# The planner's clocks, the zero products' limit and the per-stretch settings of a two-layer attention and MLP kernel

## The chip, the cores and the metric

The kernel runs on one core of one Trainium2 chip. The metric is the device time of one execution in microseconds. Four engines share the work: TensorE (PE in the profile) for matrix products, ScalarE (ACT) for exponentials and tanh, VectorE (DVE) for elementwise work, GpSimd (POOL) for integer additions. SyncE (SP) issues the DMAs.

## The reference

The input x has 2048 rows of 512 bfloat16 values. Two layers are run with the same weights. Each layer is an attention block and an MLP block, both with a residual:

```python
x = x + _A_ref(_layernorm(x, axis=-1), A_wqkv, A_wo)   # 32 heads of 16, softmax over 2048 keys
x = x + _B_ref(_layernorm(x, axis=-1), B_w1, B_w2)     # 512 -> 1792, silu, -> 512
x = x + _A_ref(_layernorm(x, axis=-1), A_wqkv, A_wo)
x = x + _B_ref(_layernorm(x, axis=-1), B_w1, B_w2)
```

Inside `_A_ref` the scores are `q k / 4`, softmax is taken over all keys, and the heads' outputs are joined and multiplied by `wo`. The heads are so narrow (16 columns) that the exponentials, 2 x 32 x 2048 x 2048 of them, are the bulk of the work.

## The kernel before, in words

**Tiles and segments.** The queries are cut into 4 chunks of 512 and the heads into 8 groups of 4 (`hb`). A segment (`Seg`) is one layer, one chunk and one group of heads. It walks over 16 blocks of 128 keys, and each block gives two tiles (`pr` 0 and 1, two heads each), so a full segment has 32 tiles. In the second layer some segments are split: an "old" part over 12 key blocks (24 tiles), which can begin before the last chunk of the first layer is finished, and a "new" part over the last 4 (8 tiles). There are 74 segments and 2048 tiles: 1024 in layer 0 (chunks 0 to 3 one after another), then 240 in "old" parts, 272 in the rest of chunks 0 and 1 of layer 1, and 512 in chunks 2 and 3 of layer 1.

**One tile.** TensorE writes the scores of a tile into one of three PSUM slots (L1282). Then one of two ways makes the exponentials. Either ScalarE does it in one activation (L1497). Or VectorE does it: one multiply-add that makes the bit pattern of a rough power of two (L1531), and three shifted copies of that pattern, whose sum smooths it. Each copy is an integer addition, done on GpSimd (L1592) or on VectorE (L1565). A ScalarE tile needs one pair of value products on TensorE (L1358), a VectorE tile four such pairs, one for each copy. The value products of a segment add up in a single PSUM bank, `o_ps`. When all are done the bank is copied out (`close`, L1176 to L1184), and only then may the next segment's value products begin. Until then its exponentials wait in SBUF buffers, of which there are 14 and some lent ones.

**Background work.** Everything else (keys, queries, values, layer norm, output projection, MLP) is cut into `Piece`s: lists of steps, each with an engine, a planned duration in ns and a function. Two pieces matter here. `k_piece` ends with `k_out`, a VectorE step that writes keys into `KT` (planned at 302 ns, L321). `heads_piece` divides the heads' outputs by their sums: after a DMA transpose of `oT` into the single buffer `at`, one VectorE step `heads_norm` issues a reciprocal of the sums (L513) and a product over all values (L514). It is planned as one step of 640 ns (one group of heads) or 920 ns (two groups). There are 42 such pieces. The kernel's `ending` calls `heads_norm` once more.

**The order.** The order of instructions on TensorE, ScalarE, VectorE and GpSimd is fixed when the program is built. Class `Flow` plays the kernel on a model: each engine has a clock (`self.pe`, `self.act`, `self.dve`, `self.pool`), the engine with the earliest clock takes a turn, and instructions are written in the order in which the model issues them. A planned duration is therefore not a time on the chip; it only changes the order. Two clocks model the waiting of VectorE and GpSimd for one another: `self.lock` is the end of GpSimd's last planned addition, `self.held_port` the end of the last VectorE step marked "l". A VectorE step marked "l" is planned not before `self.lock`, and GpSimd's next addition not before `self.held_port`.

**Which tile goes to VectorE.** `want_dve` (L1248) says so for each tile as its scores are issued. Before, only tiles issued as a pair (two free slots at once) could go; not those of the last four positions of a segment (`left < LAST`, 5); not with more than `behind` additions pending; not with fewer than `spare` free buffers; not two tiles in direct succession. Those two numbers, and others, come from a letter: `RULES` has 128 letters, one for each 16 tiles, and `KINDS` gives each letter's numbers as (spare, many, few, behind, hurry, help, wait). `help` and `wait` say when VectorE makes shifted copies itself, `hurry` scales how fast background work is fed in.

**Zero products.** Where TensorE would be idle in the plan, `warm` (L1379) inserts a product with a matrix of zeros (L1393), if the planned busy share of the last 3300 ns is at most `WARM`, 0.65. They add nothing to a result.

Of the kernel before, what the change touches and what calls it, by code (L numbers as in the profile page):

```python
# [12 lines left out]
FP32 = mybir.dt.float32  # L13
# [7 lines left out]
def kernel(  # L21
# [14 lines left out]
    S, D = xf.shape  # L36
    F = B_w1.shape[-1]
    P = 128
    H = 32
    DH = D // H  # L40
# [224 lines left out]
    def dve(ns, fn, g=""):  # L265
        return ("dve", ns, fn, g)
# [62 lines left out]
    def k_piece(L, c, hb):  # L329
        cell = {}  # L330

        def out():
            st = cell["st"] = stpool.tile([P, 512], BF16, name="kq", tag="kq")
            nc.vector.tensor_copy(out=st[:], in_=cell["ps"][:, :])  # L334
            move(kept_q[L, hb, c, :, :], st[:])

        p = Piece(four(
            lambda cts: k_mm(c, hb, cell["ps"][:, :], cts),
            lambda: bank(cell, "k_ps"),
        ) + [dve(700, out, "c"), dve(302, lambda: k_out(c, hb, cell["st"][:]), "l")])  # L340
        p.key = (L, c, hb)
        p.store = Piece([])
        return p
# [163 lines left out]
        return fetch, f  # L507


    def heads_norm(at_ps, hb, attn):  # L510
        n = at_ps.shape[2]
        rec = bmpool.tile([P, 4, 8, 1], FP32, name="rec", tag="rec")[:, :, 0:n, :]
        nc.vector.reciprocal(rec, at_ps[:, :, :, DH : DH + 1])  # L513
        nc.vector.tensor_tensor(  # L514
            out=attn[:, :, 64 * hb : 64 * hb + DH * n].rearrange("p t (j d) -> p t j d", j=n),
            in0=at_ps[:, :, :, 0:DH],
            in1=rec.to_broadcast([P, 4, n, DH]),
            op=ALU.mult,
        )

# [2 lines left out]
    def heads_piece(oT, seg, attn):  # L523
        alone = seg.c < 2 and (seg.L == 1 or seg.hb < 2)
        alone = alone or (seg.L, seg.c, seg.hb) == (1, NQC - 1, HB - 2)
        k = 0 if alone else seg.hb % 2
        if k == 0:
            at_cell["at"] = opool.tile([P, 4, 2, P], BF16, name="at", tag="at")
        at = at_cell["at"]
        turn(at[:, :, k, :], oT[:])  # L530
        if not alone and k == 0:
            return None
        n = 4 * (k + 1)
        heads = at[:].rearrange("p t s (j w) -> p t (s j) w", j=4)[:, :, 0:n, :]
        return Piece([dve(640 if k == 0 else 920, lambda: heads_norm(heads, seg.hb - k, attn))])

    def o_transpose(a_ps, attn, tq):
        for ct in range(CT):
# [115 lines left out]
    def ending(oT, attn, slots, units):  # L654
# [24 lines left out]
        for tq, k in units[4:10]:  # L679
            tail_mm(slots, tq, k)  # L680
        warm(max(0, 5 - len(units[4:])))
        heads_norm(at_ps, hb, attn)
        a_ps = gpool.tile([P, 4, P], BF16, name="a4_ps", tag="g")
        for tq in range(4):
            nc.tensor.transpose(a_ps[:, tq, :], attn[:, tq, (CT - 1) * P : D], ident[:, :])
# [117 lines left out]
    first = [0]  # L803
# [136 lines left out]
    class Flow:  # L940
# [36 lines left out]
        def rule(self, n):  # L977
            letter = RULES[n // STRETCH]
            (
                self.spare, self.many, self.few, self.behind, self.hurry, self.help, self.wait,  # L980
            ) = KINDS[letter]

        def landed(self, at):
# [262 lines left out]
            return max(self.end + 916 * (j + 1), t.at + 490 + 1017) + 50  # L1246

        def want_dve(self, t, at, two):  # L1248
            if not two or t.n < 4 or t.n - self.last_dve < 2:
                return False  # L1250
            left = 2 * len(t.seg.kts) - 2 * (t.kt - t.seg.kts[0]) - t.pr
            if left < LAST or len(self.zs) > 0 or len(self.passes) > self.behind:
                return False
            if sum(b[0] <= at + 600 for b in self.bufs) - self.owed() < self.spare:
                return False
            if sum(len(l) for l in self.lanes) > ROWS:
                return False
            return self.dve < at + 475 + LATE
# [356 lines left out]

    SWITCH, T_PASS, T_BITS, T_SHIFT = 100, 1225, 430, 1000

    LAST, ROWS, LATE, EVEN = 5, 20, 900, 0
    SPAN, WARM = 3300, 0.65
    STRETCH = 16  # L1620
    KINDS = {
        "a": (5, 6, 2, 3, 1.0, 2, 100), "b": (3, 6, 2, 3, 1.0, 2, 100), "c": (4, 6, 2, 3, 1.0, 2, 100),
        "d": (6, 6, 2, 3, 1.0, 2, 100), "e": (8, 6, 2, 3, 1.0, 2, 100), "f": (99, 6, 2, 3, 1.0, 2, 100),
        "g": (5, 4, 2, 3, 1.0, 2, 100), "h": (5, 9, 2, 3, 1.0, 2, 100), "i": (5, 6, 1, 3, 1.0, 2, 100),
        "j": (5, 6, 3, 3, 1.0, 2, 100), "k": (5, 6, 2, 2, 1.0, 2, 100), "l": (5, 6, 2, 5, 1.0, 2, 100),
        "m": (5, 6, 2, 6, 1.0, 3, 100), "n": (5, 6, 2, 6, 1.0, 3, 400), "o": (5, 6, 2, 4, 1.0, 3, 300),
        "p": (5, 6, 2, 3, 1.4, 2, 100), "q": (5, 6, 2, 3, 0.7, 2, 100), "r": (99, 6, 2, 3, 1.5, 2, 100),
        "s": (5, 6, 2, 3, 1.4, 3, 100), "t": (5, 6, 2, 3, 1.0, 3, 100), "u": (5, 6, 2, 3, 1.0, 1, 100),
        "v": (5, 6, 2, 3, 1.0, 2, 300), "w": (4, 6, 2, 6, 1.0, 3, 400), "x": (7, 6, 2, 6, 1.0, 3, 400),
        "y": (5, 4, 2, 6, 1.0, 3, 400), "z": (5, 6, 2, 6, 1.4, 3, 400), "A": (5, 9, 2, 6, 1.0, 3, 400),  # L1630
        "B": (5, 6, 2, 6, 0.7, 3, 400), "C": (5, 6, 3, 6, 1.0, 3, 400),
    }
    RULES = (
        "bbbbbbbbmmmmmmmmwwwwwwwwwwwwwwwwppppppppbbbbbbbbddddddddcccccccc"
        "aaaaaaaakkkkkkkknnnnnnnnvvvvvvvvwwwwwwwwwwwwwwwweeeeeeeellllllll"
    )
    TAU, NEAR, URGENT, HARD = 700, 300, 4000, 6000
    FROM, TO, EARLY = 0, 99, 300
# [155 lines left out]
```

## Time and profile before

| what | value |
|---|---|
| median of 3 runs | 1624.14 us (1622.63 to 1628.64) |
| time of the profiled execution | 1620.71 us |
| its span, first to last instruction | 1618.9 us |
| ACT busy, PE busy | 1557.0 us and 1546.3 us (96% each) |
| POOL busy, DVE busy | 1293.6 us (80%) and 1239.8 us (77%) |
| mean granted clock of TensorE | 0.991 |
| tiles on ScalarE (L1497) and on VectorE (L1531) | 1596 and 452 |
| shifted copies on GpSimd (L1592) and VectorE (L1565) | 1203 and 153 |
| zero products of the plan (L1393) | 211 |

Busy times are shares of the span of one execution. TensorE's matmuls overlap and their ends are modelled, so its 96% is not a measure of how full it is. An instruction's duration includes the time that it waits for a shared port, which matters for VectorE and GpSimd here. A wait is put down to the engine that released it.

### The profile page before, as it was taken

The page shows a single profiled execution, that of the slowest core. Times are in us where ns is not written, and L with a number is a line of the kernel's source. Part 1 is how long each engine was busy: PE and PEld are TensorE (multiplying, and loading weights), DVE is VectorE, ACT ScalarE, POOL GpSimd, SP SyncE. Part 2 cuts the span into 40 slices and gives each one's busy share as a digit, 9 for nine tenths or more (in the row PEclk, how much of TensorE's full clock was granted, in tenths as well). Part 3 has the DMA queues.
Part 4 walks back from the last instruction along what each step waited for, and adds up shares of the span by engine and source line. Part 5 has one row for each costly group of instructions (what it writes and reads, how often), then busy time and mean ns, then how long its engine had stood idle before and what let it go on. Part 6 is the DMA issues. An engine that isn't in the chain of part 4 may idle for free.

```text
span 1618.9 us, 41459 instructions
## 1 busy us (share of the span) xinstructions
PE 1546.3 (96%) x16750; PEld 477.4 (29%) x16756; DVE 1239.8 (77%) x1550; ACT 1557.0 (96%) x1767; POOL 1293.6 (80%) x1349
## 2 busy tenths in 40 slices
PE   8999999999999999999999999998999999999998
PEld 3322222233322323233222232222223222222333
DVE  7898888876777678658987668886878887777764
ACT  6999999999999999999999998998999999999993
POOL 3899998987898778868777866876879998889880
PEclk9999999999999999999999999998999999999999
DMA  5011101100210011001120011112100110010000
GB/s 195 21 40 37 30 23 27 27 11 11 37 23 11 11 27 41 11 14 33 57 59 23 14 27 35 37 35 45 30 11 17 33 27 14 18 33 18 17 24 14
DMA packets 105744, 49.24 MB, mean 30 GB/s; under 512 B 79024, under 2 KB 105040, under 8 KB 105552
## 3 DMA queue, kind: packets, MB, share of 16 engines
q1 hardware_dynamic: 103536, 45.51, 11.0%
q8 instruction: 131, 2.15, 0.6%
q10 hardware_dynamic: 2016, 1.08, 0.2%
q14 instruction: 61, 0.50, 0.1%
HBM read 17.20 MB, written 11.27 MB: 18 GB/s over the span
## 4 chain that ended last, share of the span: by engine, by line
PE 59%; ACT 22%; DVE 11%; issue 6%; POOL 2%; DMA 1%; ACTq 0%; DVEq 0%; POOLq 0%
PE slot L1282 21%; PE q_ps L1358 19%; ACT p L1497 15%; PE y_ps L312 7%; PE h_ps L312 4%; DVE p L1531 3%; ACT v L1497 3%; ACT t_sb L580 2%; PE k_ps L312 2%; PE v_ps L312 1%; PE q_ps L312 1%; POOL p L1592 1%; DVE hT L584 1%; PE w_ps L1393 1%; DVE kq L334 1%
## 5 line engine op out<-in xcount | busy, mean ns | idle before, releaser
L1497 ACT ACTIVATE p<-slot 128x1024 bf16<-128x1024 f32 x1168 | 1172.4, 1203 | 17.4 <-PE slot L1282 17.1
L1592 POOL TENSOR_TENSOR p<-p,steps 128x512 int32<-128x512 int32 x681 | 710.9, 1068 | 186.6 <-DVE p L1531 167.2
L1282 PE MATMUL slot<-QT,KT 32*128 32x512 bf16 x4096 | 596.6, 383 | 36.8 <-ACT p L1497 18.3
L1358 PE MATMUL q_ps<-p,v 128*17 128x512 bf16 x4956 | 566.1, 384 | 5.6 <-DVE p L1531 2.3
L1531 DVE TENSOR_SCALAR p<-slot 128x1024 uint16<-128x1024 f32 x341 | 415.5, 1219 | 106.0 <-PE slot L1282 99.9
L1282 PEld LDWEIGHTS <-KT 32*128 32x128 bf16 x4096 | 198.8, 91 | 615.9 <-issue 609.9
L1497 ACT ACTIVATE v<-slot 128x1024 bf16<-128x1024 f32 x289 | 329.3, 1211 | 1.9 <-PE slot L1282 1.9
L1358 PEld LDWEIGHTS <-v 128*17 128x17 bf16 x6808 | 157.3, 88 | 292.9 <-issue 244.1
L1358 PE MATMUL q_ps<-v,v 128*17 128x512 bf16 x1222 | 195.2, 382 | 1.2 <-POOL v L1592 0.8
L1592 POOL TENSOR_TENSOR v<-p,steps 128x512 int32<-128x512 int32 x159 | 170.4, 1081 | 23.2 <-DVE p L1531 17.1
L1592 POOL TENSOR_TENSOR p<-v,steps 128x512 int32<-128x512 int32 x123 | 130.8, 1081 | 8.4 <-DVE v L1531 8.0
L312 PE MATMUL h_ps<-xnT,w_sb 128*32 128x512 bf16 x1568 | 130.3, 384 | 6.8 <-DVE hT L584 6.6
L312 PE MATMUL y_ps<-w_sb,hT 128*32 128x512 bf16 x1568 | 121.8, 383 | 0.5 <-DVE hT L584 0.5
L584 DVE SCALAR_TENSOR_TENSOR hT<-t_sb,h_ps 128x512 bf16<-128x512 f32 x98 | 66.8, 682 | 58.2 <-ACT t_sb L580 57.9
L1531 DVE TENSOR_SCALAR v<-slot 128x1024 uint16<-128x1024 f32 x69 | 84.2, 1220 | 26.8 <-PE slot L1282 25.7
L1497 ACT ACTIVATE wkq<-slot 128x1024 bf16<-128x1024 f32 x74 | 87.2, 1215 | 0.1
L312 PE MATMUL k_ps<-xnT,wkq 128*32 128x512 bf16 x960 | 78.2, 383 | 0.0
L580 ACT ACTIVATE t_sb<-h_ps 128x512 f32<-128x512 f32 x98 | 76.0, 776 | 0.0
L421 DVE SCALAR_TENSOR_TENSOR QT<-qc,cols,q_ps 128x512 bf16<-128x512 bf16 x74 | 55.0, 743 | 21.6 <-PE q_ps L312 21.0
L1358 PE MATMUL q_ps<-wkq,v 128*17 128x512 bf16 x336 | 58.3, 387 | 0.6 <-ACT wkq L1497 0.4
L312 PEld LDWEIGHTS <-hT 128*32 128x32 bf16 x2016 | 41.0, 95 | 57.1 <-issue 40.8
L1497 ACT ACTIVATE wv_sb<-slot 128x1024 bf16<-128x1024 f32 x44 | 51.7, 1174 | 4.7 <-PE slot L1282 4.5
(168 smaller groups left out, 1469.5 us busy)
## 6 DMA issues: line engine op xcount, KB each, us to landing
qc<-kept_q SPq DMA_DIRECT2D x70, 112.0 KB, 2.0
kept_q<-kq SPq DMA_DIRECT2D x60, 128.0 KB, 1.8
w_sb<-in_B_w_dram SPq DMA_DIRECT2D x2, 1792.0 KB, 13.0
out_dram<-x_sb SPq DMA_DIRECT2D x15, 128.0 KB, 1.7
x_sb<-in_A_x_dram SPq DMA_DIRECT2D x3, 512.0 KB, 7.0
old_q<-QT SPq DMA_DIRECT2D x10, 128.0 KB, 1.7
q_was<-old_q SPq DMA_DIRECT2D x10, 128.0 KB, 2.0
at<-oT SPq DMA_TRANSPOSE x63, 2.3
```

The costliest lines, as they stand in the source:

```text
L312: nc.tensor.matmul(ps[g, :], lhsT=lhsT[:, g], rhs=rhs, start=start, stop=stop, skip_group_check=True)
L334: nc.vector.tensor_copy(out=st[:], in_=cell["ps"][:, :])
L421: nc.vector.scalar_tensor_tensor(out=dst, in0=qc[:], scalar=own, in1=ps, op0=ALU.mult, op1=ALU.add)
L580: nc.scalar.activation(t_sb, ps, ACT.Tanh, scale=0.5)
L584: nc.vector.scalar_tensor_tensor(out=hT[:, ft, :], in0=t_sb, scalar=1.0, in1=ps, op0=ALU.add, op1=ALU.mult)
L1282: nc.tensor.matmul(self.slots[k][:, jj, :], lhsT=KT[32 * j : 32 * j + KR, t.seg.hb, t.kt * P : (t.kt + 1) * P], rhs=t.seg.QT[32 * j : 32 * ...
L1358: nc.tensor.matmul(self.o_ps[32 * j : 32 * j + VW, :], lhsT=vs[seg.L][:, t.kt, 4 * seg.hb + j, :], rhs=buf[:, jj, :], start=not seg.opened ...
L1393: nc.tensor.matmul(out[0:DH, :], lhsT=wkq[rows, 0, 2 * D : 2 * D + DH], rhs=wo_sb[rows, 0, :], start=out is not self.o_ps, stop=out is not ...
L1497: nc.scalar.activation(buf[:].rearrange("p a b -> p (a b)"), self.slots[x.slot][:].rearrange("p a b -> p (a b)"), ACT.Exp, scale=float(SCALE),
L1531: nc.vector.tensor_scalar(out=whole.bitcast(U16), in0=self.slots[x.slot][:].rearrange("p a b -> p (a b)"), scalar1=float(UNIT), scalar2=fl ...
L1592: nc.gpsimd.tensor_tensor(out=b1.bitcast(I32), in0=b0.bitcast(I32), in1=steps32[:, k : k + 1].to_broadcast([P, 512]), op=ALU.add,)
```

## The change

Five edits, all in the planner or in how a step is cut:

- `heads_norm` is cut into `heads_rec` (the reciprocal) and `heads_mul` (the product). `heads_piece` makes two steps of them: 190 and 410 ns for one group, 280 and 560 ns for two, the second marked "l". `ending` calls both in a row. The instructions are the same two.
- `k_out` is planned at 350 ns, not 302.
- `WARM` is 0.70, not 0.65.
- Each letter gets two more numbers. `last` replaces the constant `LAST` of 5. `solo` lets a tile whose scores are issued alone go to VectorE, if at least `solo` tiles wait for ScalarE; with 9 that never happens, with 1 often.
- `KINDS` is written anew, and `RULES` too. What each range of tiles gets is in the table below; the order of numbers is (spare, behind, hurry, help, wait, last, solo), `many` and `few` being 6 and 2 everywhere.

| tiles | before | after |
|---|---|---|
| 0-127 | 3, 3, 1.0, 2, 100, 5, - | 4, 3, 1.0, 2, 100, 5, - |
| 128-255 | 5, 6, 1.0, 3, 100, 5, - | 4, 3, 1.0, 2, 100, 5, - |
| 256-511 | 4, 6, 1.0, 3, 400, 5, - | the same |
| 512-639 | 5, 3, 1.4, 2, 100, 5, - | 5, 6, 1.0, 3, 400, 3, 1 |
| 640-767 | 3, 3, 1.0, 2, 100, 5, - | 5, 6, 1.0, 3, 400, 3, 1 |
| 768-895 | 6, 3, 1.0, 2, 100, 5, - | 4, 6, 1.0, 3, 400, 5, - |
| 896-1023 | 4, 3, 1.0, 2, 100, 5, - | 5, 3, 1.0, 2, 100, 5, 1 |
| 1024-1151 | 5, 3, 1.0, 2, 100, 5, - | 5, 3, 1.0, 2, 100, 8, - |
| 1152-1279 | 5, 2, 1.0, 2, 100, 5, - | 5, 3, 1.0, 2, 100, 8, - |
| 1280-1407 | 5, 6, 1.0, 3, 400, 5, - | 5, 5, 1.0, 2, 100, 5, - |
| 1408-1535 | 5, 3, 1.0, 2, 300, 5, - | 5, 5, 1.0, 2, 100, 5, - |
| 1536-1791 | 4, 6, 1.0, 3, 400, 5, - | 5, 3, 1.4, 2, 100, 3, - |
| 1792-1919 | 8, 3, 1.0, 2, 100, 5, - | 5, 3, 1.4, 2, 100, 5, - |
| 1920-2047 | 5, 5, 1.0, 2, 100, 5, - | 5, 3, 1.0, 2, 100, 5, 1 |

```diff
-        ) + [dve(700, out, "c"), dve(302, lambda: k_out(c, hb, cell["st"][:]), "l")])
+        ) + [dve(700, out, "c"), dve(350, lambda: k_out(c, hb, cell["st"][:]), "l")])
...
-    def heads_norm(at_ps, hb, attn):
-        n = at_ps.shape[2]
-        rec = bmpool.tile([P, 4, 8, 1], FP32, name="rec", tag="rec")[:, :, 0:n, :]
+    def heads_rec(at_ps):
+        m, n = at_ps.shape[1:3]
+        rec = bmpool.tile([P, 4, 8, 1], FP32, name="rec", tag="rec")[:, 0:m, 0:n, :]
         nc.vector.reciprocal(rec, at_ps[:, :, :, DH : DH + 1])
+        return rec
+
+    def heads_mul(at_ps, rec, hb, attn):
+        m, n = at_ps.shape[1:3]
         nc.vector.tensor_tensor(
             out=attn[:, :, 64 * hb : 64 * hb + DH * n].rearrange("p t (j d) -> p t j d", j=n),
             in0=at_ps[:, :, :, 0:DH],
-            in1=rec.to_broadcast([P, 4, n, DH]),
+            in1=rec.to_broadcast([P, m, n, DH]),
...
-        return Piece([dve(640 if k == 0 else 920, lambda: heads_norm(heads, seg.hb - k, attn))])
+        cell = {}
+
+        def first():
+            cell["rec"] = heads_rec(heads)
+
+        def second():
+            heads_mul(heads, cell["rec"], seg.hb - k, attn)
+
+        return Piece([dve(190 if k == 0 else 280, first), dve(410 if k == 0 else 560, second, "l")])
...
-        heads_norm(at_ps, hb, attn)
+        heads_mul(at_ps, heads_rec(at_ps), hb, attn)
...
                 self.spare, self.many, self.few, self.behind, self.hurry, self.help, self.wait,
+                self.last, self.solo,
...
-            if not two or t.n < 4 or t.n - self.last_dve < 2:
+            if not two and len(self.exps) < self.solo or t.n < 4 or t.n - self.last_dve < 2:
                 return False
             left = 2 * len(t.seg.kts) - 2 * (t.kt - t.seg.kts[0]) - t.pr
-            if left < LAST or len(self.zs) > 0 or len(self.passes) > self.behind:
+            if left < self.last or len(self.zs) > 0 or len(self.passes) > self.behind:
...
-    LAST, ROWS, LATE, EVEN = 5, 20, 900, 0
-    SPAN, WARM = 3300, 0.65
+    ROWS, LATE, EVEN = 20, 900, 0
+    SPAN, WARM = 3300, 0.7
...
     RULES = (
-        "bbbbbbbbmmmmmmmmwwwwwwwwwwwwwwwwppppppppbbbbbbbbddddddddcccccccc"
-        "aaaaaaaakkkkkkkknnnnnnnnvvvvvvvvwwwwwwwwwwwwwwwweeeeeeeellllllll"
+        "ccccccccccccccccxxxxxxxxxxxxxxxxFFFFFFFFFFFFFFFFxxxxxxxxCCCCCCCC"
+        "GGGGGGGGGGGGGGGGkkkkkkkkkkkkkkkkttttttttttttttttqqqqqqqqCCCCCCCC"
     )
```

## The prediction

> **What bounds the kernel now.** I read the page's busy shares first, then the groups of instructions, then the same work by ranges of tiles, then the waits and the granted clock.
>
> The page, engines and costliest groups:
>
> ```profile
> PE 1546.3 (96%) x16750; PEld 477.4 (29%) x16756; DVE 1239.8 (77%) x1550; ACT 1557.0 (96%) x1767; POOL 1293.6 (80%) x1349
> ...
> L1497 ACT ACTIVATE p<-slot 128x1024 bf16<-128x1024 f32 x1168 | 1172.4, 1203 | 17.4 <-PE slot L1282 17.1
> L1592 POOL TENSOR_TENSOR p<-p,steps 128x512 int32<-128x512 int32 x681 | 710.9, 1068 | 186.6 <-DVE p L1531 167.2
> ```
>
> ScalarE is the bound. Over all its buffers L1497 sat idle for only 24.7 us (17.4 + 1.9 + 0.1 + 4.7 + 0.6, from the groups), the opening and the ending take some 32 and 43 us of the 1618.9 us span, and between them one exponential follows another: in the timeline five start at 1071.93 us and the next at 1076.51 us, 0.92 us each. So the time is the number of tiles left to ScalarE, 1596, times 0.92, and little else. A tile more for VectorE is 0.92 us less, as long as GpSimd and VectorE have room. GpSimd has: its additions waited 167.2 us for a VectorE tile to be made.
>
> Windows cut at each 128th tile (us, ACT and POOL busy of all work first; then L1531 alone, whose x is the count of VectorE tiles):
>
> ```profile
> 695.30:792.60 97.30, 95.61 (x1156) 30.16 (x1155) 73.14 (x91) 97.30 (x108) 69.91 (x78) 1.00 0.12 34
> 1097.10:1203.60 106.50, 97.74 (x954) 28.32 (x954) 79.65 (x100) 100.03 (x114) 83.06 (x85) 0.94 0.14 30
> 1203.60:1292.70 89.10, 88.64 (x1039) 26.30 (x1035) 75.04 (x85) 89.08 (x101) 80.94 (x77) 1.00 0.11 25
> ```
>
> ```profile
> 695.30:792.60 97.30, 28.03 (x23) 1.00 0.12 34
> 1203.60:1292.70 89.10, 40.22 (x33) 1.00 0.11 25
> ```
>
> The same 128 tiles took 97.3 us with 23 VectorE tiles and 89.1 us with 33: ten tiles, 8.2 us, which is 0.92 each less the tanh work that ScalarE has in the second. The range from 1097 us is the dear one: ScalarE is not full and the granted clock (the column after POOL) is 0.94.
>
> The clock in it, and before two shorter falls (windows of all engines; PE is the first number after the length):
>
> ```profile
> 241.50:245.00 3.50, 3.23 (x22) 0.92 (x20) 2.03 (x3) 3.50 (x5) 3.44 (x4) 1.00 0.16 38
> 245.00:248.40 3.40, 3.40 (x26) 0.57 (x28) 1.55 (x2) 2.48 (x4) 2.87 (x4) 0.50 0.01 2
> 600.00:603.40 3.40, 3.40 (x22) 0.44 (x18) 2.57 (x3) 2.80 (x3) 3.12 (x4) 0.50 0.14 30
> 1115.40:1125.60 10.20, 9.29 (x52) 1.80 (x50) 5.88 (x8) 4.87 (x6) 5.83 (x7) 0.50 0.10 24
> ```
>
> Five stretches, 27 us in all (3.4, 3.4, 6.8, 10.2, 3.4; also 1077.8 and 1132.4 us), run at half clock, and in each ScalarE goes idle. How the longest began, from the timeline:
>
> ```profile
> 1112.88 1.07 DVE L514 TENSOR_TENSOR attn<-at,rec 128x256 bf16<-128x256 bf16 x1
> ...
> 1113.87 1.21 DVE L1531 TENSOR_SCALAR p<-slot 128x1024 uint16<-128x1024 f32 x1
> ...
> 1115.13 0.40 PE L1282 MATMUL slot<-QT,KT 32*128 32x512 bf16 x2 [1.05 <-DVE p L1531]
> ...
> 1121.88 1.02 ACT L1497 ACTIVATE wv_sb<-slot 128x1024 bf16<-128x1024 f32 x1 [3.53 <-PE slot L1282]
> ```
>
> A heads' product took 1.07 us, the VectorE tile behind it came late, TensorE stood 1.05 us for its slot, the clock fell, and the next query tile, made at half clock, kept ScalarE idle for 3.53 us.
>
> **The change part by part.**
>
> *Heads' product and `k_out`.* No instruction is added. The group rows by form show the product at 890 ns (256 columns) and 1162 ns (512) on average, with a least of 467 ns over all 42, and the reciprocal at 243 and 343 ns. Together that is 1.13 and 1.51 us against the planned 0.64 and 0.92: 21 x 0.49 + 21 x 0.59 = 22.7 us of VectorE time that the plan did not know of, 0.54 us at each of 42 places. Now the plan lets the product wait for GpSimd. Queued behind it on VectorE are the next VectorE tile, the copy of `o_ps` and the query chain; behind it on SP stands the transpose into the single `at`, for which SP waited 19.1 us in 6 cases, 3.6 at most. What of the 22.7 us reaches ScalarE is seen only where the order is tight: the two ranges from 999 to 1204 us (tiles 1280-1535) hold 204.2 us with 55 VectorE tiles, of which ScalarE was busy 193.3. Those 10.9 us idle are the upper bound of the gain. The lower bound is a loss: VectorE's clock in the plan now runs 0.54 us later 42 times, and at the worst each place loses a third of a VectorE tile, 42 x 0.3 x 0.3 = 4 us as an estimate. I take -3, nearer to the one stall that I can show (3.5 us). `k_out` is planned 48 ns longer 60 times against a measured 759 on average: nothing to see, hidden under the 77% of VectorE.
>
> *Zero products at 0.70.* Of 211 now. They go only where the plan has TensorE idle, at 0.215 us each (in the timeline one alone stands as 0.38 us, three in a row as 0.81). By the starts of the matmuls in the timeline I count some 100 windows of 3.4 us whose streaming share lies between 0.60 and 0.70, so I expect about 90 more. In the way of scores they cost between 0 and 20 us (all 90); they stand where the plan has TensorE waiting, so I take 0.5, two or three of them. The gain is the idle time of ScalarE in the five slow stretches: 0.92 + 1.03 + 1.92 + 5.23 + 0.47 = 9.6 us, from its gaps. Streaming shares before the first three were 0.64, 0.58 and 0.55, before the others 0.43 and 0.49; five hundredths more can lift only the first three, 3.9 us. I take -3.5, together -3 (bounds -9.6 and +20).
>
> The Trainium skill ("TensorE: Matmul & The Clock Gate", Part 1, the HAM clock gate) has the clock fall to half only after at least one idle window of about 3.4 us. The 3.4 us steps and the half agree with the trace. The idle window does not: in the 3.4 us before 245.0 us the profile has TensorE busy for 3.23. By that rule more zero products would cure nothing, and the sum below would be 3.5 us higher.
>
> *Settings.* Counted by range of tiles, from L1531 in windows. Where the old numbers had `behind` 6 and `help` 3 with `wait` 400 (256-511, 1280-1407, 1536-1791), 128 tiles held 32, 28, 28, 33 and 32 VectorE tiles; elsewhere 23 to 32. Tiles 512-767 get these numbers, with `last` 3 and `solo` 1: 57 now, and about 62 then (GpSimd is idle for 31 us of 189 there, room for nine tiles at 3 x 1.07). 768-895: 27, +1.5. 896-1023 with `solo`: 23, +2. In the timeline about 740 of the scores' turns are of one tile alone, 738 tiles that could not go to VectorE before, some 40 in each such range, so `solo` opens much, but GpSimd's room decides. 1024-1279 with `last` 8 loses three positions of 24: 49, -2. 1280-1535: 55, 0. 1536-1791 goes from `behind` 6 to 3, with `last` 3: 65, -2. The rest +1. Sum +5.5 tiles, -5.1 us at 0.92. Bounds: every range above the middle one's 28 falls to it (-19 tiles, +17 us), or every range below 32 rises to it (+61 tiles, 56 us; they need 61 x 3 x 1.07 = 196 us of GpSimd, which is idle for 263 of the 1544.6 us of the ranges; with half of them, -28 us).
>
> *Late tiles.* `last` 3 lets VectorE take a tile three from the end, in 16 segments (512-767, 1536-1791). Its chain is 0.53 + 1.22 + 3 x 1.07 = 5.0 us; where the last VectorE tile stood six or more from the end, `o_ps` was copied out 4.1 us after the last scores on average. The wait is covered by the free buffers; without them ScalarE stops. I take 0, bounds 0 and +26 (below).
>
> Sum: -3 - 3 - 5.1 = -11.1 us. Against the profiled execution, 1620.7, that is 1609.6. The median of the runs lies 3.4 above that execution, so 1613.
>
> **The rivals.**
>
> *An even trade.* The new numbers only move VectorE tiles from one range to another. For it: GpSimd was busy 88 of 95.5 us in 1664-1791, which is nearly full. Against it: it was idle for 26 to 34 us in each of the three ranges from 695 to 999 us. Time: with the two small gains halved 1621, between 1616.5 and 1630.
>
> *Slower: late tiles hold up the segments.* In the 16 segments with `last` 3 the copy of `o_ps` moves from 4.1 us to 5 or more, exponentials pile up in the buffers, and ScalarE stops. Idle gaps of ScalarE now are 1.08, 1.38, 3.53 and 4.02 us where something like it happened: 2.5 on average, 16 x (2.5 - 0.92) = +25 us, against -11 from the rest: 1638. It decides from about 1.6 us idle at each border, where the 16 x (1.6 - 0.92) eat the 11. For it: segments whose last VectorE tile stood five or fewer from the end were copied out after 4.6 to 5.9 us on average. Against it: from tile 1536 on more buffers are lent.
>
> *The clock isn't cured.* Shares of 0.65 and 0.70 are the same to the gate, since TensorE never stands for 3 us outside the opening. Then the zero products only cost 0.5: 1613 + 3.5 = 1616.5. This is what the Trainium skill's rule in "TensorE: Matmul & The Clock Gate", Part 1, would make of it. The falls after shares of 0.64 and 0.58 speak against it, that windows of about 0.48 (811.5 and 1429.3 us) were followed by none speaks for it.
>
> **How the numbers follow.** A change under 0.5% (8.1 us: 1616.0 to 1632.3) is about what a measurement of this kernel can't tell from none. My forecast has 0.44, with a range of its own of 1600 to 1617; the even trade 0.20; the late tiles 0.28, 1626 to 1650; the clock not cured 0.08. Faster: 0.40 + 0.02 + 0.00 + 0.04 = 0.46. Same: 0.04 + 0.17 + 0.02 + 0.04 = 0.27. Slower: 0.00 + 0.01 + 0.26 + 0.00 = 0.27. The range of 1598 to 1638 leaves out some 0.06 below and the upper half of the late tiles above.
>
> **What would show it.** L1531 at about 457 (x summed over its rows), most of the growth between tiles 512 and 1023; L1393 at about 300; no half clock near 245, 600 and 1078 us of the old work; tiles 1280-1535 in less than 204 us. I am wrong if L1531 falls under 445, if L1497's idle time rises over 35 us, or if gaps of ScalarE stand at the borders of the 16 segments.

## The result and the profile after

The changed kernel is a little slower: 1632.82 us median (1628.24 to 1637.22, 12 runs) against 1622.31 (1619.67 to 1628.64, 12 runs), a ratio of 1.0052 [1.0036, 1.0068] (the plain quotient of the two medians is 1.0065). The forecast was 1613. The profiled execution took 1628.24 us (span 1626.5, 7.6 us more than before's) at a mean granted clock of 0.990, and is the fastest of the twelve; their mean clock is 0.9866, against 0.990 for the kernel before.

The page of the kernel after, engines and the two groups that answer to those shown of before:

```profile
PE 1562.8 (96%) x16867; PEld 485.7 (30%) x16873; DVE 1221.0 (75%) x1556; ACT 1558.9 (96%) x1768; POOL 1282.8 (79%) x1339
...
L1510 ACT ACTIVATE p<-slot 128x1024 bf16<-128x1024 f32 x1188 | 1184.7, 1195 | 21.2 <-PE slot L1295 20.4
L1605 POOL TENSOR_TENSOR p<-p,steps 128x512 int32<-128x512 int32 x650 | 682.6, 1073 | 203.0 <-DVE p L1544 178.4
```

ScalarE is still the bound. Over all buffers VectorE makes 451 tiles, one fewer than before, and the exponentials on ScalarE wait 28.3 us instead of 24.7. Those are 0.9 and 3.6 us. ScalarE's remaining rise in busy time (1.9 us in all, tile included) and the opening and the ending, 0.8 and up to 1 us longer, make most of the rest. GpSimd waits for tiles even longer than before (178.4 us in this group).

The new settings moved tiles, as windows cut at each 128th tile show (after; tiles 768-895, 896-1023, 1024-1151, 1152-1279, 1408-1535; columns as before):

```profile
593.90:690.40 96.50, 94.84 (x1042) 29.01 (x1041) 75.44 (x91) 96.50 (x112) 80.92 (x87) 1.00 0.11 26
690.40:792.20 101.80, 99.67 (x1162) 31.18 (x1161) 74.24 (x94) 97.41 (x108) 75.93 (x82) 0.97 0.09 24
792.20:894.80 102.60, 98.56 (x1107) 31.08 (x1106) 81.56 (x113) 99.95 (x112) 66.85 (x71) 0.98 0.17 48
894.80:1001.80 107.00, 102.43 (x1172) 33.73 (x1169) 67.33 (x89) 103.75 (x118) 62.16 (x70) 1.00 0.09 24
1099.10:1203.80 104.70, 99.94 (x950) 29.07 (x947) 78.30 (x97) 98.35 (x112) 81.06 (x84) 0.97 0.14 30
```

The same, VectorE's tiles alone (L1544, the old L1531), for tiles 896-1023, 1024-1151 and 1152-1279:

```profile
690.40:792.20 101.80, 31.71 (x26) 0.97 0.09 24
792.20:894.80 102.60, 26.84 (x22) 0.98 0.17 48
894.80:1001.80 107.00, 25.69 (x21) 1.00 0.09 24
```

| tiles | before: us, VectorE tiles | after | forecast of VectorE tiles |
|---|---|---|---|
| 0-511 | 375.2, 115 | 374.0, 116 | 116 |
| 512-767 | 189.3, 57 | 187.7, 60 | 62 |
| 768-895 | 99.4, 27 | 96.5, 28 | 28.5 |
| 896-1023 | 97.3, 23 | 101.9, 26 | 25 |
| 1024-1279 | 206.8, 49 | 209.6, 43 | 47 |
| 1280-1535 | 204.2, 55 | 202.0, 53 | 55 |
| 1536-1791 | 184.7, 65 | 187.3, 64 | 63 |
| 1792-2047 | 188.3, 61 | 191.9, 61 | 61 |

A range's time also holds the tanh work and the copies that the plan puts there, so rows move by more than their tiles. Range 896-1023 got three tiles more and is 4.5 us longer: before, ScalarE was busy for all of its 97.3 us, and now for 97.41 of 101.80. The granted clock of 0.97 there leads to one of the stretches at half speed (all engines, after; three of them):

```profile
744.20:751.00 6.80, 6.80 (x44) 1.05 (x40) 4.21 (x6) 5.12 (x5) 5.83 (x7) 0.50 0.27 60
1082.10:1085.50 3.40, 3.15 (x28) 0.67 (x27) 1.13 (x3) 2.25 (x3) 1.04 (x1) 0.50 0.72 79
1450.70:1457.50 6.80, 6.80 (x54) 1.08 (x50) 4.49 (x6) 4.88 (x6) 5.34 (x6) 0.50 0.00 0
```

In each of the two of 6.8 us ScalarE was busy for about 5. In this profile the old stretches at 245 and 600 us are gone. The one at 1078 us is not: where the kernel before was at half clock from 1077.8 to 1084.6 us, this one is from 1082.1 to 1085.5. Others stand at 10.3 (in the opening), 744.2, 795.4, 1126.5, 1136.7 and 1450.7 us: 34.4 us at half clock in all, against 31.1 before (the end of the kernel counted in both). That is with 346 zero products instead of 211. The clock differs from run to run of one program, so a single stretch in a single profile proves little.

The heads' product, by shape (after):

```profile
L518 DVE TENSOR_TENSOR attn<-at,rec 128x512 bf16<-128x512 bf16 x21 | 22.4, 1066 | 0.5
L518 DVE TENSOR_TENSOR attn<-at,rec 128x256 bf16<-128x256 bf16 x21 | 22.2, 1055 | 0.5
```

It was 1162 and 890 ns. The plan lets it wait for GpSimd now, but on the chip it takes as long as before on average (1.06 us against 1.03). A likely reason, not shown, is that the plan and the chip aren't at the same place when it is issued.

### The profile page after: what moved, and what is told of

Same layout as the page of the kernel before. It is cut to its first block, busy times and chain, and to the rows that moved or that the text cites. A ratio compares the mean times of both kernels' runs of the same rounds, so it can differ in the third digit from the quotient of the medians.

```text
span 1626.5 us, 41692 instructions
## 1 busy us (share of the span) xinstructions
PE 1562.8 (96%) x16867; PEld 485.7 (30%) x16873; DVE 1221.0 (75%) x1556; ACT 1558.9 (96%) x1768; POOL 1282.8 (79%) x1339
## 4 chain that ended last, share of the span: by engine, by line
PE 64%; ACT 21%; DVE 8%; issue 5%; POOL 1%; DMA 1%; ACTq 0%; DVEq 0%; SPq 0%; POOLq 0%
PE slot L1295 22%; PE q_ps L1371 20%; ACT p L1510 12%; PE y_ps L312 7%; PE h_ps L312 4%; ACT v L1510 3%; PE k_ps L312 3%; ACT t_sb L592 2%; DVE p L1544 2%; PE q_ps L1406 2%; PE v_ps L312 1%; ACT wv_sb L1510 1%; PE q_ps L312 1%; PE w_ps L1406 1%; DVE hT L596 1%
## 5 line engine op out<-in xcount | busy, mean ns | idle before, releaser
L1510 ACT ACTIVATE p<-slot 128x1024 bf16<-128x1024 f32 x1188 | 1184.7, 1195 | 21.2 <-PE slot L1295 20.4
L1605 POOL TENSOR_TENSOR p<-p,steps 128x512 int32<-128x512 int32 x650 | 682.6, 1073 | 203.0 <-DVE p L1544 178.4
L1544 DVE TENSOR_SCALAR p<-slot 128x1024 uint16<-128x1024 f32 x319 | 389.2, 1220 | 126.2 <-PE slot L1295 116.5
L1510 ACT ACTIVATE v<-slot 128x1024 bf16<-128x1024 f32 x271 | 303.7, 1215 | 2.8 <-PE slot L1295 2.6
L1605 POOL TENSOR_TENSOR v<-p,steps 128x512 int32<-128x512 int32 x153 | 162.0, 1068 | 20.6 <-DVE p L1544 16.7
L1544 DVE TENSOR_SCALAR v<-slot 128x1024 uint16<-128x1024 f32 x77 | 94.1, 1221 | 28.3 <-PE slot L1295 22.6
L1406 PE MATMUL q_ps<-wo_sb,wkq 128*16 128x512 bf16 (+1 forms) x270 | 91.8, 380 | 0.0
L1510 ACT ACTIVATE wkq<-slot 128x1024 bf16<-128x1024 f32 x63 | 73.8, 1203 | 2.3 <-PE slot L1295 2.3
L1605 POOL TENSOR_TENSOR p<-wkq,steps 128x512 int32<-128x512 int32 x56 | 59.9, 1086 | 13.1 <-PE f_ps L312 5.1
L1510 ACT ACTIVATE wv_sb<-slot 128x1024 bf16<-128x1024 f32 x56 | 64.0, 1186 | 2.0 <-PE slot L1295 2.0
```

The lines of the kernel that those rows point to most:

```text
L1406: nc.tensor.matmul(out[0:DH, :], lhsT=wkq[rows, 0, 2 * D : 2 * D + DH], rhs=wo_sb[rows, 0, :], start=out is not self.o_ps, stop=out is not ...
L1510: nc.scalar.activation(buf[:].rearrange("p a b -> p (a b)"), self.slots[x.slot][:].rearrange("p a b -> p (a b)"), ACT.Exp, scale=float(SCALE),
L1544: nc.vector.tensor_scalar(out=whole.bitcast(U16), in0=self.slots[x.slot][:].rearrange("p a b -> p (a b)"), scalar1=float(UNIT), scalar2=fl ...
L1605: nc.gpsimd.tensor_tensor(out=b1.bitcast(I32), in0=b0.bitcast(I32), in1=steps32[:, k : k + 1].to_broadcast([P, 512]), op=ALU.add,)
```

## The experiments

Two theories are set against each other. *Local*: each part has its own small price (a dearer range here, a clock there), and the parts add up. *Fit*: the 128 letters fit one exact order, in which a few deadlines are just met; anything that changes a planned number redraws the order, and the cost is the stalls at those deadlines, whatever the edit was for. The expectations name them by letters. Z, S, K and D are forms of the local theory: the zero products, the settings or the truer clocks carry the price, or each part its own. F is the fit. F was formed only after the first four runs, of which the first three had come out above every range expected.

### Each part alone

**The zero products' limit alone**, on the kernel before:

```diff
-    SPAN, WARM = 3300, 0.65
+    SPAN, WARM = 3300, 0.7
```

> The kernel before with the zero products' limit at 0.70 alone. Theory Z (the added zero products stand ahead of real products on TensorE and cost the time): L1393 rises from 211 to about 300 and the time by 5 to 10 us, to a ratio of 1.003 to 1.006. Theory S (the letters cost it, the zero products nothing): ratio 0.997 to 1.001, with as many half-clock stretches or fewer. My prediction's own sizes: -3 us, 0.998.

Measured: 1656.83 us, 1.0201 [1.0179, 1.0224]. It has 401 zero products and 459 VectorE tiles, seven more than before, its mean clock is higher (0.992), and it is 2% slower. Windows of this run, then of the kernel before, over tiles 1024-1151 and 1152-1279:

```profile
799.10:913.70 114.60, 109.69 (x1084) 31.80 (x1083) 86.43 (x117) 97.14 (x107) 71.20 (x74) 0.91 0.15 42
913.70:1041.90 128.20, 119.72 (x1283) 39.90 (x1280) 72.54 (x93) 103.20 (x119) 70.72 (x79) 0.97 0.08 20
```

```profile
792.60:892.90 100.30, 95.04 (x1055) 29.75 (x1052) 82.49 (x111) 98.30 (x111) 73.77 (x79) 1.00 0.16 41
892.90:999.40 106.50, 101.05 (x1174) 32.23 (x1171) 71.79 (x92) 101.64 (x115) 72.24 (x79) 1.00 0.09 24
```

The two ranges take 14.3 and 21.7 us more, and ScalarE is busy for hardly more of them (97 and 103 us, against 98 and 102). The first 896 tiles end 0.6 us later with 42 zero products more (695.9 us against 695.3), which speaks against the products themselves as the price. What grew is ScalarE's idle time. Its two longest gaps (timeline of this run):

```profile
799.59 2.86 ACT L1497 ACTIVATE p<-slot 128x1024 bf16<-128x1024 f32 x3 [8.31 <-PE slot L1282]
...
1021.27 1.02 ACT L1497 ACTIVATE p<-slot 128x1024 bf16<-128x1024 f32 x1 [17.45 <-PE slot L1282]
```

The first gap stands before the first "old" segment of layer 1. It ends as the first window above begins, and makes the range ahead of that window 5.9 us longer. The second stands before the first "new" segment, whose keys come from the last chunk of layer 0. In the first window itself the gaps are shorter (5.1, 3.1 and 2.3 us at most), and TensorE ran 20.5 us of it at half clock, where the kernel before ran none.

**The clocks alone** (the split product marked "l", and `k_out`), on the kernel before:

```diff
-dve(302, lambda: k_out(c, hb, cell["st"][:]), "l")
+dve(350, lambda: k_out(c, hb, cell["st"][:]), "l")
...
-        return Piece([dve(640 if k == 0 else 920, lambda: heads_norm(heads, seg.hb - k, attn))])
+        return Piece([dve(190 if k == 0 else 280, first), dve(410 if k == 0 else 560, second, "l")])
```

> The kernel before with the reciprocal and the product of the heads as two steps, the second waiting for GpSimd in the plan, and keys planned at 350 ns; limit 0.65 and letters of before. Theory K (truer clocks make the plan give VectorE fewer tiles): 440 to 447 VectorE tiles where there were 452, ratio 1.003 to 1.007. Theory S and theory Z: 450 to 454 VectorE tiles and a ratio of 0.997 to 1.002. My prediction's size: -3 us, 0.998.

Measured: 1657.60 us, 1.0194 [1.0174, 1.0215]. 448 VectorE tiles, exponentials idle for 57.5 us; the largest losses are at tiles 1152-1279 (+13.5 us) and 1408-1535 (+8.7).

**The settings alone**, with the old clocks and 0.65 (the letters' numbers in `KINDS` are those of the change too, left out here):

```diff
-            if not two or t.n < 4 or t.n - self.last_dve < 2:
+            if not two and len(self.exps) < self.solo or t.n < 4 or t.n - self.last_dve < 2:
...
-            if left < LAST or len(self.zs) > 0 or len(self.passes) > self.behind:
+            if left < self.last or len(self.zs) > 0 or len(self.passes) > self.behind:
...
-        "bbbbbbbbmmmmmmmmwwwwwwwwwwwwwwwwppppppppbbbbbbbbddddddddcccccccc"
-        "aaaaaaaakkkkkkkknnnnnnnnvvvvvvvvwwwwwwwwwwwwwwwweeeeeeeellllllll"
+        "ccccccccccccccccxxxxxxxxxxxxxxxxFFFFFFFFFFFFFFFFxxxxxxxxCCCCCCCC"
+        "GGGGGGGGGGGGGGGGkkkkkkkkkkkkkkkkttttttttttttttttqqqqqqqqCCCCCCCC"
```

> The letters of after, with last and solo, on the clocks and the limit of before. Theory S: VectorE tiles move from the range after 1024 to that before it, none are won, and the ratio is 1.003 to 1.008 as in the whole change. Theory Z and theory K: ratio 0.996 to 1.001, since the letters won tiles up to 1023 (+8 in the whole change).

Measured: 1645.21 us, 1.0119 [1.0097, 1.0142], with 449 VectorE tiles and a loss at 1024-1279 again (+6.0 and +14.5 us).

**All but the 0.70**, on the kernel after:

```diff
-    SPAN, WARM = 3300, 0.7
+    SPAN, WARM = 3300, 0.65
```

> The whole change but with the limit at 0.65. Theory Z: the ratio to the kernel before falls from 1.005 to 0.998 to 1.001, with about 211 zero products and less time at half clock. Theory S: it stays at 1.004 to 1.008, and more half-clock stretches than the 31 us of after would show that the zero products did help.

Measured: 1635.70 us, 1.0063 [1.0041, 1.0085]. Against the whole change (1.0052) the limit makes no difference that these runs can tell, though alone it cost 2.0%. In the same way the settings cost 1.2% on the old clocks, and on the new ones they gain 1.3% (1.0194 to 1.0063). The three parts alone add up to 5.1%, together they cost 0.5%. So the parts don't add up, as the local theory needs them to: a changed planned number has no fixed price of its own here.

### How little is enough

**One nanosecond.** The planned duration of `k_out`, on the kernel before:

```diff
-dve(302, lambda: k_out(c, hb, cell["st"][:]), "l")
+dve(303, lambda: k_out(c, hb, cell["st"][:]), "l")
```

> The kernel before with the planned time of the key step at 303 ns where it was 302. No instruction is slower or faster for it; only the order can change. Theory F (the letters of before fit one exact plan, in which the query tiles of layer 1 come just in time; whatever changes the plan draws the stalls anew): ratio 1.005 to 1.015, the loss as idle time of ScalarE at the first old segment (near 795 us) and the first new one (near 1000 us), with 452 or more VectorE tiles. Theory D (each part of the change costs by what it does): ratio 0.998 to 1.002.

Measured: 1646.89 us, 1.0152 [1.0129, 1.0174]. What differs is the order and which tiles go to VectorE, 456 instead of 452. Exponentials idle for 51.4 us. Tiles 1152-1279 take 120.0 us, 13.5 more than before. The timeline of this run, the chain from the last chunk's values over keys to the first query tile of the "new" segment:

```profile
992.74 0.69 DVE L379 CAST v<-v_ps 128x512 bf16<-128x512 f32 x1 [1.24 <-PE v_ps L312]
993.48 1.05 PE L312 MATMUL k_ps<-xnT,wkq 128*32 128x512 bf16 x16 [0.16 <-DVE v L379]
994.58 0.69 DVE L334 CAST kq<-k_ps 128x512 bf16<-128x512 f32 x1 [1.15 <-PE k_ps L312]
...
998.03 0.75 DVE L421 SCALAR_TENSOR_TENSOR QT<-qc,cols,q_ps 128x512 bf16<-128x512 bf16 x1 [1.08 <-PE q_ps L312]
998.83 0.61 PE L1282 MATMUL slot<-QT,KT 32*128 32x512 bf16 x6 [0.85 <-DVE QT L421]
999.32 1.02 ACT L1497 ACTIVATE p<-slot 128x1024 bf16<-128x1024 f32 x1 [14.39 <-PE slot L1282]
```

The same chain in the kernel before:

```profile
976.16 0.69 DVE L379 CAST v<-v_ps 128x512 bf16<-128x512 f32 x1 [0.92 <-PE v_ps L312]
...
978.00 0.69 DVE L334 CAST kq<-k_ps 128x512 bf16<-128x512 f32 x1 [1.15 <-PE k_ps L312]
...
980.88 0.75 DVE L421 SCALAR_TENSOR_TENSOR QT<-qc,cols,q_ps 128x512 bf16<-128x512 bf16 x1 [0.51 <-PE q_ps L312]
...
992.47 1.02 ACT L1497 ACTIVATE p<-slot 128x1024 bf16<-128x1024 f32 x1 [4.02 <-PE slot L1282]
```

From the last copy of values to the query tile it is 4.7 us before and 5.3 here: the chain is hardly slower. It begins 16.6 us later, and ScalarE has no other tile left. The same place in other runs (start of the last copy of values of that chunk, and the largest gap of ScalarE behind it):

| run | last copy of values at | largest gap |
|---|---|---|
| kernel before | 976.16 | 4.02 |
| kernel after | 979.71 | 2.41 |
| all but the 0.70 | 986.68 | 0.19 |
| limit 0.60 alone (below) | 992.43 | 2.30 |
| one nanosecond | 992.74 | 14.39 |
| clocks alone | 999.59 | 8.54 |
| settings alone | 1000.10 | 12.82 |
| limit 0.70 alone | 1014.27 | 17.45 |
| letter G with `last` 5 (below) | 1005.73 | 22.59 |

So the order hangs on a deadline. Of the six edits in this table that cost over 1%, five miss it by 8 to 23 us of idle ScalarE. It isn't the whole price: the limit of 0.60 loses 1.25% and misses it by no more than the kernels before and after do, and the whole change but the 0.70 has no gap there and is still at 1.0063.

**The limit downward**, 0.60 on the kernel before:

```diff
-    SPAN, WARM = 3300, 0.65
+    SPAN, WARM = 3300, 0.6
```

> The kernel before with the zero products' limit at 0.60, fewer zero products. Theory D, with zero products that stand in the way: ratio 0.995 to 1.000. Theory F: ratio 1.004 to 1.012, with the idle time of ScalarE in the same two places as in the run with 0.70.

Measured: 1644.07 us, 1.0125 [1.0102, 1.0149]; 182 zero products, 68.4 us at half clock (mean clock 0.9845), exponentials idle for 51.0 us (the profile is of the slowest of the six runs). Tiles 1024-1151 take 110.6 us, 10.3 more than before, but 1152-1279 hardly more, where the fit had expected the second loss. Idle time and half clock both rose, so this run alone doesn't tell the theories apart; with the run at 0.70 it shows that the limit loses in both directions.

**Letter G**, which the change puts on tiles 1024-1279, with 5 in place of 8:

```diff
-"G": (5, 6, 2, 3, 1.0, 2, 100, 8, 9),
+"G": (5, 6, 2, 3, 1.0, 2, 100, 5, 9),
```

> The whole change, but letter G (tiles 1024 to 1279) with last 5 instead of 8. My prediction's reading (last 8 only gives VectorE tiles away, two of them): 1 to 4 more VectorE tiles there and 1 to 4 us less than after, a ratio of 1.003 to 1.005. Theory F: that letter holds the deadline of the query tiles; without it ScalarE stands idle for 25 to 40 us between 790 and 1030 us and the ratio is 1.018 to 1.030.

Measured: 1662.48 us, 1.0251 [1.0228, 1.0273]. VectorE gets five tiles more in the two ranges (48 for 43), and they take 110.9 and 131.3 us for 102.6 and 107.0. That fits a letter chosen to keep VectorE free for the chain. But one nanosecond does 13 us at this place too, so the run shows that the letter belongs to its order, not that the three positions as such are worth 32 us.

### The zero products, with the order kept

The one way to price them is to leave the plan alone. Here products are issued where the planned share is over 0.65 and, with those added counted in, not over 0.70; the plan's clocks don't learn of them, so every other instruction keeps its place:

```diff
             if t + MM > limit or self.share(t) > (HOT if idle else WARM):
+                if t + MM <= limit and not idle:
+                    self.more(t)
                 return False
```

> The kernel before with its order kept and about 105 zero products more, put where the share is below 0.70, without the plan's clocks moving. It shows what zero products themselves do. My prediction's term: 3.5 us gained and 0.5 paid, ratio 0.997 to 0.999, and fewer than 27 us at half clock. Zero products in the way: 1.002 to 1.010, up to 20 us. No effect: 0.999 to 1.001.

Measured: 1619.90 us, 0.9975 [0.9960, 0.9989]: 0.25%, which is 4 us gained. From the groups of this run, the products added:

```profile
L1414 PE MATMUL q_ps<-wo_sb,wkq 128*16 128x512 bf16 (+1 forms) x105 | 40.6, 387 | 0.0
```

and the place where the longest fall of before was (all engines, this run, which is some 2 us later there):

```profile
1115.40:1125.60 10.20, 8.25 (x74) 2.29 (x72) 8.29 (x12) 8.96 (x11) 8.97 (x9) 1.00 0.16 39
```

TensorE is at full clock there, with 74 matmuls in 8.25 us where it had 52 in 9.29, and ScalarE is busy for 8.96 us of 10.2 where it was for 4.87. Time at half clock fell from 31.1 to 20.2 us in the two profiles; over all runs the mean clock rose from 0.990 to 0.994. The falls at 1078, 1115 and 1132 us are gone in this profile and one of 3.4 us at 1023 is new. Those at 245 and 600 us stand, the second for 10.2 us instead of 3.4:

```profile
244.80:248.20 3.40, 3.40 (x26) 0.48 (x24) 0.78 (x1) 2.79 (x4) 3.09 (x4) 0.51 0.17 38
599.80:610.00 10.20, 10.20 (x63) 1.73 (x59) 5.83 (x6) 7.18 (x8) 6.94 (x7) 0.50 0.16 39
```

**The same up to 0.80** (292 products added):

```diff
-            if self.share(t) + added > 0.70 or t < self.pe_extra:
+            if self.share(t) + added > 0.80 or t < self.pe_extra:
```

> The kernel before, its order kept, with zero products up to a share of 0.80, some 290 more where 0.70 gave 105. If the gain goes on with the clock: ratio 0.994 to 0.997 and a granted clock near 0.998. If by now they stand in the way of scores: 0.998 to 1.006, with more idle time of ScalarE for the slots at a full clock.

Measured: 1625.44 us, 1.0011 [0.9997, 1.0026], mean clock 0.992. The gain is gone, and so is half of the clock.

### Letters fitted anew

If the letters fit one order, then other letters should do for the new clocks what the old ones did for theirs. First, letters chosen so that the plan's last exponential comes early, on the old clocks, on the new clocks (limit 0.65), and on the old clocks with 87 zero products added. Apart from these clocks and products only `RULES` differs from the kernel after: the letters' numbers are those of the change. For the first:

```diff
-        "bbbbbbbbmmmmmmmmwwwwwwwwwwwwwwwwppppppppbbbbbbbbddddddddcccccccc"
-        "aaaaaaaakkkkkkkknnnnnnnnvvvvvvvvwwwwwwwwwwwwwwwweeeeeeeellllllll"
+        "ttttttttkkkkkkkkxxxxllllBBBBBBBBhhCCwwqqffffccnnbbbbbbbbllllEEEE"
+        "aaaaGGDDuuuujjEEzzzznnkkppppllllrrrrFFFFppBBqqqqllllllllttyymmmm"
```

> The clocks and the limit of before, with last and solo, and letters that were chosen anew by playing the plan until its own end stopped falling (11 more VectorE tiles, 463, and little waiting for query tiles). Theory F (what counts is that the letters fit the plan that they run in): ratio 0.990 to 0.996, with 460 or more VectorE tiles and 20 to 30 us of idle ScalarE in the ranges. If the chip doesn't follow the plan that finely: 0.997 to 1.005.

> The clocks of after, the limit of before (0.65), letters chosen anew in the same way and for about as long (454 VectorE tiles). Theory F: ratio 0.992 to 0.999, well under the 1.0052 of the whole change. If the truer clocks are worth something in themselves (my prediction's -3 us), it comes out no slower than the run with the clocks of before, although it has 9 tiles fewer; if not, 4 to 9 us slower than that run.

> The same letters on the clocks of before, and 87 zero products more with the order kept, as in the run that added zero products to the kernel before. If the two effects add up: 3 to 5 us under the run without them, ratio 0.987 to 0.994 to the kernel before, mean granted clock 0.993 or more.

Measured: 1633.98 us, 1.0069 [1.0044, 1.0094]; 1629.64 us, 1.0034 [1.0019, 1.0048]; 1640.11 us, 1.0107 [1.0080, 1.0134]. These miss. The first has 463 VectorE tiles, and its last exponential came at 1572.9 us, 3.6 earlier than before's; but from there to the end it took 59.3 us instead of 42.4. The letters had pushed MLP work past the last exponential. The fit was judged by the wrong event. The 87 zero products gained nothing on this order: 1640.11 us against 1633.98, at a mean clock of 0.9875 against 0.990.

So the choice was made again, by the plan's last piece of work: two sets on the old clocks, one on the new clocks (0.65), and the first set with 105 zero products added. The first two sets:

```diff
-        "bbbbbbbbmmmmmmmmwwwwwwwwwwwwwwwwppppppppbbbbbbbbddddddddcccccccc"
-        "aaaaaaaakkkkkkkknnnnnnnnvvvvvvvvwwwwwwwwwwwwwwwweeeeeeeellllllll"
+        "EEEEEEEEffuuxxxxzzzzppppxxxxzzzzCCCCFFFFiiiiiiiiddddhhggDDDDCCtt"
+        "ddllddddwwyykkkkkkkkppzzttxxttjjEEEEllFFhhooAAAADDDDDDDDnnppbbvv"
```

```diff
+        "bbbbbbbbuuuuuuuuxxvvxxxxBBBBBBBBhhCCwwqqffffbbbbbbbbbbbbllllEEff"
+        "ggCCGGDDGGGGGGGGwwwwwwwwwwwwuuuuxxxxkkkkttttttttddddddddCCCCCCCC"
```

> Clocks and limit of before, letters chosen anew by the plan's last piece of work (459 VectorE tiles, no work left over at the end). Theory F: 452 tiles become 459, 6.4 us, and the ending is back at 42 to 44 us: ratio 0.994 to 0.999. If the chip's luck with the plan of before counts for more than 7 tiles: 1.000 to 1.006.

> The same clocks and limit, another set of letters (451 VectorE tiles, hardly any waiting for query tiles in the plan). Theory F: ratio 0.996 to 1.001, ScalarE idle between tiles 1024 and 1535 for under 10 us where before has 18. If the chip's luck with the plan of before counts for more: 1.002 to 1.007.

> The clocks of after, limit 0.65, letters chosen anew in the same way and for as long (446 VectorE tiles). If truer clocks are worth what I predicted (-3 us): no slower than the runs on the clocks of before. If they only make the plan more careful, so that it gives VectorE fewer tiles: 13 tiles fewer than the first of those, 4 to 12 us slower than it, ratio 1.000 to 1.006 to the kernel before.

> The first of these with about 105 zero products more and its order kept. If added zero products do here what they did to the kernel before (0.9975): 2 to 6 us under the run without them, ratio 0.991 to 0.997, with a mean granted clock 0.002 to 0.005 higher.

Measured, beside 28 runs of the kernel before (1623.95):

| run | median us | ratio | VectorE tiles | mean clock |
|---|---|---|---|---|
| old clocks, first set | 1617.29 | 0.9953 [0.9933, 0.9974] | 459 | 0.992 |
| old clocks, second set | 1614.63 | 0.9936 [0.9913, 0.9960] | 451 | 0.993 |
| new clocks | 1628.58 | 1.0033 [1.0014, 1.0051] | 446 | 0.986 |
| first set, 105 zero products | 1618.02 | 0.9965 [0.9946, 0.9984] | 459 | 0.9925 |

After the last exponential the first two take 42.9 and 43.7 us, about as long as before's 42.4.

The second set beats both kernels with as many VectorE tiles as the changed one, 451. Its page and its exponentials:

```profile
PE 1537.4 (96%) x16727; PEld 484.5 (30%) x16727; DVE 1224.9 (76%) x1531; ACT 1556.6 (97%) x1768; POOL 1306.5 (81%) x1364
...
L1498 ACT ACTIVATE p<-slot 128x1024 bf16<-128x1024 f32 x1174 | 1173.8, 1208 | 7.5 <-PE slot L1283 7.1
```

ScalarE does the same work (1556.6 us busy, 1557.0 before), and its exponentials wait 11.9 us in all instead of 24.7. The span is 12.2 us shorter, 1606.7: this profile is the luckiest of seven runs at a clock of 0.997, so the size of the median's gain, 9 us, is the safer one. The mean clock of the seven is 0.993 against 0.990, and by the slope given at the end that goes with some 3 of the 9 us. Between the opening and the last exponential no gap of ScalarE reaches 1.5 us, and at the deadline the last copy of values begins at 967.25 us, 8.9 earlier than before.

On the new clocks the letters found in the same way end 0.8 to 1.0% later than on the old ones, with a lower clock and fewer VectorE tiles. Truer clocks didn't make a better order here. A few sets are thin evidence for that as a rule. The zero products gained nothing on the first set: the two intervals overlap, and the clock is the same (0.9925 against 0.992).

## Why the prediction was wrong

The forecast was 1613, the result 1632.8. It lies inside the range of 1598 to 1638, but on the slower side, and not by the mechanism that was given for that side.

- *ScalarE is the bound, a VectorE tile more is 0.92 us less.* True as a price of a tile, not as a forecast of the time: the limit of 0.70 alone has seven tiles more and loses 33 us, the second fitted set has one tile fewer than before and gains 9. What differs is idle time of ScalarE, 58.3 and 11.9 us against 24.7.
- *The sum of three local terms is the step that failed.* In the changed kernel none of the three came. The settings' 5.5 tiles more, -5.1 us, came out as one tile fewer, +0.9. The heads' product, -3, waits as long as before. The zero products, -3, go with 34.4 us at half clock instead of 31.1. And as parts alone, "heads' product and `k_out`, -3" and "zero products at 0.70, -3" are +1.94% and +2.01% as changes of the plan. Their bounds, up to +4 and +20, left out what follows from how the kernel is made: a planned duration changes only the order, and so all of it. The +31 and +33 us are the order, with single gaps of 8 to 17 us where before had 4.0 at most.
- *Zero products, the mechanism.* Near in size, not in place. With the order of before kept, 105 of them gained 4 us (3.5 less 0.5 forecast) and the mean clock rose by 0.004. But the forecast's gain was that of the first three falls, at 245, 600 and 1078 us, and of these only the third is gone in that run's profile. The last two, at 1115 and 1132 us, which the prediction had thought out of reach, are gone as well (ScalarE idle for 1.2 us of the 10.2 at 1115 instead of 5.3). So the share of TensorE before a fall did not tell which fall would go, and the agreement in size is in part luck. On two other orders such products gained nothing. The count was forecast at about 300; it was 346, since the order is another. The rival "the clock isn't cured" falls for the order of before alone. The rule of the Trainium skill ("TensorE: Matmul & The Clock Gate", Part 1) that the clock falls to half after an idle window of about 3.4 us doesn't account for these falls: between the opening and the end the profile of the kernel before has TensorE idle for no longer than 1.05 us at a time. In the changed kernel itself no cure shows: its order has falls of its own.
- *Heads' product.* The idea that the product, planned to wait, would find GpSimd done failed: 1.06 us on average against 1.03.
- *Settings, +5.5 tiles, -5.1 us.* The tiles were one fewer. Tiles 512-767, 768-895, 896-1023 and 1536-1791 were within two of the forecast, but the dear part was mis-sized: 1024-1279 lost six tiles for two, and 1280-1535 two for none. That is the rival of the even trade, whose tiles were right (452 to 451) and whose time of 1621 was 12 us too low: it had kept half of the small gains, and instead idle time rose and the clock fell. What `last` 8 is for I had read as a loss of three positions only.
- *Late tiles, 0, bounds to +26.* Right: tiles 512-767 with `last` 3 took 187.7 us for 189.3 (1536-1791 took 2.7 more, with one tile fewer), and in the changed kernel only two gaps of 2 us or more stand anywhere after the opening, at 792.76 and 995.12 us, neither of them in the 16 segments. The slower side came by another way than the rival that was given for it.
- *What would show it.* The count of L1531's tiles was 451, not 457, idle time of L1497 at 28.3 (under the 35 named), no borders with gaps, tiles 1280-1535 at 202.0 as said. Of the old half-clock places 245 and 600 us were free, 1078 was not. None of the signs named for being wrong appeared: they looked for one large mishap, and the loss is 0.9 us of tiles, 3.6 of idle time, some 1.5 at the two ends, and a lower clock in most runs.

Why the parts, each bad alone, cost only 0.5% together: the new letters fit the new clocks better than the old ones do, as far as the runs go (settings +1.2% on the old clocks, -1.3% on the new). Left open are how one nanosecond in the plan comes to start the last chunk's values 16.6 us later, why nine of the twelve runs after have a lower clock than the profiled one's 0.990, how much of the standing of the kernel before is the luck of one order, and why zero products gained on one order and not on two others.

## What to carry to other kernels

Where an order is written by a planner and its settings were fitted to it, a change of any planned number is a new order: price it by the deadlines that are just met (look for the segment whose inputs come last and for the largest gap there), not by the sum of its local effects, and put the chance of a loss high. To learn what an edit is worth in itself, keep the order and add only the edit, as with the zero products here; to judge a new plan, fit the settings again for both sides and measure the end of all work, not the end of the busiest engine. After that a small gain can be real: the refit of the old plan gave 0.64% [0.40, 0.87] with 451 VectorE tiles for 452. Three of the five sets of letters fitted here came out slower than the kernel before, so a refit needs several tries.

## What the runs showed of the hardware that was not expected

- One nanosecond in a planned duration, which changes the order and sends four more tiles to VectorE, moved the time by 1.5% [1.3, 1.7].
- The granted clock differs from run to run of one and the same program, and the time goes with it: over 78 runs of the kernel before the clock lay between 0.985 and 0.997, and each 0.001 of it went with 0.97 us. By that slope, as an estimate, some 3 us of what the changed kernel lost go with the clock (0.9866 against 0.990); what sets it from run to run no run here shows.
- TensorE fell to half clock five times in the kernel before, though by the profile it stood idle for no longer than 1.05 us at a time between the opening and the end.
- More work for TensorE did not raise its clock reliably. On the order of before 105 small zero products brought the mean from 0.990 to 0.994, 292 of them to 0.992; on two other orders 87 and 105 of them left it at 0.9875 (0.990 without them) and 0.9925 (0.992).
